# Attention backward for one query row: dq by 512-column matmuls in four column groups, with a diagonal pick

## The chip, the cores and the metric

One Trainium2 chip, one core of it, one launch. The metric is device time in microseconds (us). The kernel before takes 645.75 us, the median of three timed runs (645.3 to 645.95). Durations of single instructions come from one more execution that the hardware profiler recorded.

## The reference, cut to what matters

For each of 32 heads there is one query row q (128 numbers), 8192 rows of K and of V (128 numbers each, bfloat16), and one gradient row g. The kernel returns the output and the three gradients:

```
p  = softmax(K q * d^-0.5)          # 8192 numbers
o  = V^T p                          # 128 numbers
ds = p * (V g - g.o) * d^-0.5       # 8192 numbers
dq = K^T ds                         # 128 numbers  <- the change is here
dk = ds (x) q ,  dv = p (x) g       # 8192 x 128 each, written out
```

K and V are read once (134 MB in all) and dk and dv are written once (134 MB). There is little arithmetic for each byte.

## The kernel before, in words

The 8192 rows of a head lie on 128 partitions with 64 slots of 128 numbers each (`NT` = 64), so K of a head is one tile of 128 x 8192 bfloat16, 2 MB. One DMA loads it (line 74), one loads V (L78), and one each stores dk and dv (L225, cut in two for the first and last head). All of these are issued by SyncE (SP), in order, on one queue. K has three buffers, V two, the tiles G_dk and G_dv two each; so a load or a store that needs a buffer waits on SP for the last reader of that buffer, and everything behind it on SP waits too.

The order of the instructions on each engine is the order of the program (a manual schedule). Iteration h of the loop at L260 works on the scores of head h and ends head h-1. On TensorE (PE) it goes: L230 spreads the rows q and g over the partitions; L157 multiplies K, transposed by VectorE (DVE, L146), with q (64 weight loads of 128 columns and 64 matmuls); then come 32 matmuls of dq of head h-1 (L205, from `dq_of`, L245); L173 (`s_swap`) moves the scores into their order with four fp32 matmuls, each into its own 32 partitions; then the other 32 matmuls of dq; L288 transposes the maxima; L188 transposes V in four batches of eight; L300 sums the softmax; L205 (second use) multiplies V with p; L200 multiplies the transposed V with g; L320 computes g.o.

dq of a head is thus 64 pairs: a slot of K (128 x 128) is loaded as weights, and one column of ds streams past it, all 64 summed in column 128 of the PSUM tile `dp`. ScalarE (ACT) copies that column to `dq_all` (L249). ACT also computes the exponential (L299), copies p four times over (L309), and copies the transposed V out of PSUM (L179).

DVE transposes K (L146, four of 1.2 us), computes ds (L239, L241), masks the scores (L163), and builds dk and dv (L215, four pieces of 1.2 us each). `ds` and `p` are kept four times over (R = 4 copies side by side), since L215 reads them so; the tile `ds_rep` is 128 x 64 x 4. The pieces of dv of head h (first in L324) need p, which needs the sum from L300; ds of head h (L241, in the next iteration) needs L200 and L320.

Which instruction frees which buffer: the second half of dq (L278) is the last reader of K of head h-1, and load_k (L281) stands behind it; the transposes, the products with p and L200 free V, and load_v (L327) stands behind them. The PSUM tile `dp` has two buffers (`psD`, L57).

Of the kernel before, what the change touches and what calls it, by code (L numbers as in the profile page):

```python
# [9 lines left out]
ALU = mybir.AluOpType  # L10
AX = mybir.AxisListType
BF16 = mybir.dt.bfloat16
F32 = mybir.dt.float32
PSUM = bass.MemoryType.PSUM

CH = 16
R = 4
K_BUFS = 3
V_BUFS = 2
QD = 32  # L20
# [3 lines left out]
def kernel(  # L24
# [11 lines left out]
    nc = tc.nc  # L36
    P = 128
    _, H, S, D = k.shape
    assert D == P and S % (P * CH) == 0 and H <= P
    NT = S // P  # L40
    NCH = NT // CH
    NQ = P // QD
# [5 lines left out]
    consts = ctx.enter_context(tc.tile_pool(name="consts", bufs=1))  # L48
# [5 lines left out]
    small = ctx.enter_context(tc.tile_pool(name="small", bufs=2))  # L54
    psT = ctx.enter_context(tc.tile_pool(name="psT", bufs=2, space=PSUM))
    psS = ctx.enter_context(tc.tile_pool(name="psS", bufs=1, space=PSUM))
    psD = ctx.enter_context(tc.tile_pool(name="psD", bufs=2, space=PSUM))  # L57
    psM = ctx.enter_context(tc.tile_pool(name="psM", bufs=1, space=PSUM))

    Kt, Vt, XK, XV, st = {}, {}, {}, {}, {}  # L60

    def rows_of(x, h, c, parts):
        L = NT // parts
        return x[0, h].rearrange("(p n) d -> p n d", p=P)[:, c * L:(c + 1) * L, :]

    def slots(X, c, parts):
        L = NT // parts
        return X[:, c * L:(c + 1) * L, :]

    def load_k(h):  # L70
        Kt[h] = kpool.tile([P, NT, D], BF16, tag="K", name="Kt")
        parts = NCH if h == 0 else 1
        for c in range(parts):
            nc.sync.dma_start(slots(Kt[h], c, parts), rows_of(k, h, c, parts))
# [38 lines left out]
    nc.vector.reduce_sum(lane[:], ident[:].rearrange("p (a i) -> p i a", a=NQ), axis=AX.X)  # L113
    ident_f = consts.tile([P, P], F32)
    nc.vector.tensor_copy(ident_f[:], ident[:])
    for c in range(2 * NB):
        nc.vector.tensor_tensor(
            q_blk[:, :, c, :], tp[:, c, 0:H].unsqueeze(2).to_broadcast([P, H, NQ]),
            in_quad[:].unsqueeze(1).to_broadcast([P, H, NQ]), op=ALU.mult)
# [19 lines left out]
    dq_all = consts.tile([P, H], F32)  # L139

    def k_blocks(h, u):


        if u == 0:
            XK[h] = ktpool.tile([P, CH, NB, NCH, QD], F32, tag="XK", name="XK_sb")
        nc.vector.transpose(XK[h][:, :, :, u, :],  # L146
                            slots(Kt[h], u, NCH).rearrange("p g d -> p (g d)").bitcast(F32).rearrange(
                                "p (g w j) -> p g w j", g=CH, w=NB))

    def k_scores(h):  # L150
        x = st[h]
        out = x["s"][:, 0:NT].rearrange("p (a g) -> p g a", a=NQ)
        cols = XK.pop(h).rearrange("p g w u i -> p (g w u i)").bitcast(BF16).rearrange(
            "p (g w ui e) -> p g w e ui", g=CH, w=NB, e=2)
        for g in range(CH):
            for c in range(2 * NB):
                nc.tensor.matmul(out[:, g, :], lhsT=cols[:, g, c // 2, c % 2], rhs=q_blk[:, h, c, :],  # L157
                                 start=(c == 0), stop=(c == 2 * NB - 1), skip_group_check=True)
# [44 lines left out]
    def contract(Xt, rep, out_col, first=0, last=NT):  # L203
        for n in range(first, last):
            nc.tensor.matmul(out_col, lhsT=Xt[:, n, :], rhs=rep[:, n, 0:1],  # L205
                             start=(n == 0), stop=(n == NT - 1), skip_group_check=True)

    def outer(h, which, r):
        x = st[h]
        if r == 0:  # L210
            x[which] = gpool.tile([P, NT, D], BF16, tag=which, name="G_" + which)
        G, dst = x[which], out_2 if which == "dk" else out_3
        rep, row = x["ds"] if which == "dk" else x["p"], x["qd"][:, 0 if which == "dk" else 1, :]
        Q = NT // 4
        nc.vector.tensor_tensor(  # L215
            slots(G, r, 4).rearrange("p n (a b) -> p n a b", b=R),
            slots(rep, r, 4).unsqueeze(2).to_broadcast([P, Q, D // R, R]),
            row.rearrange("p (a b) -> p a b", b=R).unsqueeze(1).to_broadcast([P, Q, D // R, R]),
            op=ALU.mult)
        parts = 1  # L220
        if h == 0 or h == H - 1:
            parts = 2
        if r % (4 // parts) == 4 // parts - 1:
            c = r // (4 // parts)
            nc.sync.dma_start(rows_of(dst, h, c, parts), slots(G, c, parts))  # L225

    def rows_bc(h):
        x = st[h]
        x["s"] = psS.tile([P, 512], F32, tag="s", name="s_ps")
        nc.tensor.matmul(x["s"][:, 256:512], lhsT=ident[0:H, h:h + 1].to_broadcast([H, P]),  # L230
                         rhs=rows[:].rearrange("h a d -> h (a d)"), start=True, stop=True,
                         skip_group_check=True)
        x["qd"] = small.tile([P, 2, D], BF16, tag="qd", name="qd")
        nc.scalar.copy(x["qd"][:].rearrange("p a d -> p (a d)"), x["s"][:, 256:512])  # L234
# [8 lines left out]
            in1=x["p_s"][:].unsqueeze(2).to_broadcast([P, NT, R]), op0=ALU.subtract, op1=ALU.mult)  # L243

    def dq_of(h, half):  # L245
        out = st[h]["dp"][:, 128:129]
        contract(Kt[h], st[h]["ds"], out, half * NT // 2, (half + 1) * NT // 2)
        if half == 1:
            nc.scalar.copy(dq_all[:, h:h + 1], out)  # L249

    def result(src, dst):
        half = small.tile([P, H], BF16, tag="half", name="half")
# [7 lines left out]
    for h in range(H + 1):  # L260
        p_ = h - 1
        if h < H:
            x = st[h] = {}
            rows_bc(h)
            for u in range(NCH):
                k_blocks(h, u)
            k_scores(h)
        if h == 0:
            do_columns()
        if h > 0:  # L270
            ds_of(p_)
            outer(p_, "dk", 0)
            dq_of(p_, 0)
        if h < H:
            s_mask(h)
            s_swap(h)
        if h > 0:
            dq_of(p_, 1)  # L278
            outer(p_, "dk", 1)
        if 0 < h and h + 2 < H:  # L280
            load_k(h + 2)  # L281
        if h < H:
            mx = small.tile([P, 1], F32, tag="mx")
            nc.vector.reduce_max(mx[:], x["sn"], axis=AX.X)
            top = small.tile([P, 1], F32, tag="top")
            nc.vector.tensor_scalar_mul(top[:], mx[:], scale)
            x["m"] = psM.tile([P, 512], F32, tag="m", name="m_ps")
            nc.tensor.transpose(x["m"][:, 128:256], top[:].to_broadcast([P, P]), ident_f[:])  # L288
        if h > 0:
            outer(p_, "dk", 2)  # L290
        if h == 0:
            load_k(2)
        if h < H:
            nbias = small.tile([P, 1], F32, tag="nbias")
            nc.vector.tensor_reduce(nbias[:], x["m"][:, 128:256], axis=AX.X, op=ALU.max, negate=True)  # L295
            v_transposes(h, 0, copy=False)
            e = small.tile([P, NT], F32, tag="e")
            rs = small.tile([P, 1], F32, tag="rs")
            nc.scalar.activation(e[:], x["sn"], ACT.Exp, bias=nbias[:], scale=scale, accum_out=rs[:])  # L299
            nc.tensor.matmul(x["m"][:, 0:1], lhsT=ones_f[:], rhs=rs[:], start=True, stop=True,  # L300
                             skip_group_check=True)
        if h > 0:
            outer(p_, "dk", 3)
        if h == H:
            break
        rinv = small.tile([P, 1], F32, tag="rinv")
        nc.vector.reciprocal(rinv[:], x["m"][:, 0:1])  # L307
        x["p"] = small.tile([P, NT, R], BF16, tag="prep", name="p_rep")
        nc.scalar.activation(x["p"][:], e[:].unsqueeze(2).to_broadcast([P, NT, R]), ACT.Copy, scale=rinv[:])  # L309
        x["p_s"] = small.tile([P, NT], F32, tag="p_s", name="p_s")  # L310
        nc.vector.tensor_scalar(x["p_s"][:], e[:], rinv[:], scale, op0=ALU.mult, op1=ALU.mult)
        v_copy(h, 0)
        v_transposes(h, 1)
        v_transposes(h, 2)
        contract(Vt[h], x["p"], x["m"][:, 2:3])
        nc.scalar.copy(o_all[:, h:h + 1], x["m"][:, 2:3])
        v_scores(h, 0)
        v_scores(h, 1)
        v_transposes(h, 3)
        nc.tensor.matmul(x["m"][:, 1:2], lhsT=do_f[:, h:h + 1].to_broadcast([P, P]), rhs=o_all[:, h:h + 1],  # L320
                         start=True, stop=True, skip_group_check=True)
        v_scores(h, 2)
        v_scores(h, 3)
        outer(h, "dv", 0)  # L324
        outer(h, "dv", 1)
        outer(h, "dv", 2)
        if 0 < h and h + 2 < H:  # L327
            load_v(h + 2)
        outer(h, "dv", 3)
        if h == 0:  # L330
            load_v(2)
        if h == H - 1:
            result(o_all, out_0)
# [33 lines left out]
```

## Time and profile before

| what | value |
|---|---|
| three timed runs | 645.3, 645.75, 645.95 us |
| span of the profiled execution (first to last instruction) | 644.6 us |
| what lies around the span, against the median | about 1.15 us |
| busy: PE, PE weight load, DVE, ACT | 482.0, 443.9, 505.9, 180.7 us |
| TensorE clock granted, mean | 0.601 of full |
| bytes moved by DMA | 269.80 MB, mean 419 GB/s |
| dq: matmuls (L205 on `dp`) | 2048, 64.0 us busy |
| dq: weight loads (L205 on `Kt`) | 2048, 59.5 us busy |
| dq: copies (L249) | 32, 159 ns each |

The page does not give a time of the profiled execution beyond its span; the difference to the timed runs is taken as constant here. Busy times of PE are unions of overlapping instructions, so 2048 matmuls of 165 ns make 64 us and not 338. "Idle before" in a row is time in which the engine stood still just before such an instruction, and what ended it. "Landing" of a DMA is when its last byte is reported.

### The profile page before, as it was taken

How to read it: one execution, taken by the hardware profiler on the slowest of the kernel's cores; microseconds unless marked ns; L12 is line 12 of the kernel's file. 1: busy time of each engine (PE TensorE's matmuls, PEld its weight loads, DVE VectorE, ACT ScalarE, POOL GpSimd, SP SyncE). 2: the span in 40 equal slices, each digit the busy share in tenths (PEclk: the TensorE clock that was granted, in tenths of full speed). 3: DMA queues.
4: the chain of work that ended last, by engine and by line, in shares of the span. 5: the costliest groups of instructions: out<-in, count | busy, mean ns of one | idle time of the engine just before them, and what ended most of it. 6: DMA issues, size and time to landing. Idle time of an engine off the chain costs nothing.

```text
span 644.6 us, 20935 instructions
## 1 busy us (share of the span) xinstructions
PE 482.0 (75%) x9673; PEld 443.9 (69%) x9673; DVE 505.9 (78%) x653; ACT 180.7 (28%) x332; POOL 0.7 (0%) x6
## 2 busy tenths in 40 slices
PE   3998898886777877768776787677876777877780
PEld 2887788785676766768666687567776676866670
DVE  5999899767977679867788777787767986778761
ACT  2333333322233231333222332123322233231230
POOL 0000000000000000000000000000000000000000
PEclk9666666665566655666556665566665566655665
DMA  8999999999999999999999999999999999999985
GB/s 350 404 428 429 424 427 424 428 429 421 418 429 428 428 425 430 430 426 431 425 428 428 430 426 428 428 428 427 427 429 431 424 432 424 430 426 429 427 362 244
DMA packets 19718, 269.80 MB, mean 419 GB/s; under 512 B 2352, under 2 KB 2352, under 8 KB 2864
## 3 DMA queue, kind: packets, MB, share of 16 engines
q1 hardware_dynamic: 19584, 268.47, 98.2%
q8 instruction: 75, 1.23, 0.7%
q14 instruction: 11, 0.09, 0.0%
q10 hardware_dynamic: 48, 0.01, 0.0%
HBM read 134.23 MB, written 134.23 MB: 416 GB/s over the span
## 4 chain that ended last, share of the span: by engine, by line
DMA 62%; PE 24%; DVE 9%; ACT 1%; issue 1%; SPq 0%; DVEq 0%; ACTq 0%
DMA Vt<-in_v_dram 61%; PE T_ps L188 15%; DVE XK_sb L146 4%; DVE G_dv L215 4%; PE m_ps L205 3%; PE dp_ps L200 2%; PE s_ps L157 2%; PE dp_ps L205 1%; DVE G_dk L215 1%; DMA Kt<-in_k_dram 1%; PE m_ps L300 1%; ACT p_rep L309 0%; PE s_ps L173 0%; ACT XT_sb L179 0%; PE m_ps L288 0%
## 5 line engine op out<-in xcount | busy, mean ns | idle before, releaser
L188 PE MATMUL T_ps<-ident_f,Vt 128*128 128x128 f32 x1024 | 217.0, 383 | 27.3 <-DMA Vt<-in_v_dram 24.7
L188 PEld LDWEIGHTS T_ps<-ident_f,Vt 128*128 128x128 f32 x1024 | 182.2, 206 | 45.2 <-PE m_ps L288 21.7
L215 DVE TENSOR_TENSOR G_dv<-p_rep,qd 128x2048 bf16<-128x2048 bf16 x128 | 148.2, 1220 | 60.9 <-DMA out_dram<-G_dv 52.8
L215 DVE TENSOR_TENSOR G_dk<-ds_rep,qd 128x2048 bf16<-128x2048 bf16 x128 | 155.6, 1218 | 4.6 <-DMA out_dram<-G_dk 3.6
L146 DVE STREAM_TRANSPOSE XK_sb<-Kt 128x1024 f32<-128x1024 f32 x128 | 148.3, 1214 | 5.8 <-DMA Kt<-in_k_dram 3.2
L179 ACT COPY XT_sb<-T_ps 128x1024 f32<-128x1024 f32 x128 | 128.7, 1008 | 83.9 <-PE T_ps L188 77.2
L157 PE MATMUL s_ps<-q_blk,XK_sb 128*128 128x4 bf16 x2048 | 59.8, 168 | 94.6 <-DVE pdt L239 87.6
L157 PEld LDWEIGHTS <-XK_sb 128*128 128x128 bf16 x2048 | 57.1, 104 | 103.9 <-DVE pdt L239 96.6
L200 PE MATMUL dp_ps<-do_blk,XT_sb 128*128 128x2 bf16 x2048 | 67.0, 164 | 18.0 <-ACT XT_sb L179 17.6
L200 PEld LDWEIGHTS <-XT_sb 128*128 128x128 bf16 x2048 | 65.5, 103 | 20.7 <-ACT XT_sb L179 20.2
L205 PE MATMUL dp_ps<-ds_rep,Kt 128*128 128x1 bf16 x2048 | 64.0, 165 | 0.4 <-DVE ds_rep L241 0.4
L205 PEld LDWEIGHTS <-Kt 128*128 128x128 bf16 x2048 | 59.5, 104 | 5.7 <-issue 5.6
L249 ACT COPY dq_all<-dp_ps 128x1 f32<-128x1 f32 x32 | 5.1, 159 | 205.2 <-PE dp_ps L205 182.8
L205 PEld LDWEIGHTS <-Vt 128*128 128x128 bf16 x2048 | 57.0, 96 | 0.7
L205 PE MATMUL m_ps<-p_rep,Vt 128*128 128x1 bf16 x2048 | 56.5, 163 | 0.0
L309 ACT ACTIVATE p_rep<-e,rinv 128x256 bf16<-128x256 f32 x32 | 16.3, 508 | 64.6 <-DVE rinv L307 64.6
L307 DVE RECIPROCAL rinv<-m_ps 128x1 f32<-128x1 f32 x32 | 5.4, 168 | 35.2 <-PE m_ps L300 35.1
L234 ACT CAST qd<-s_ps 128x256 bf16<-128x256 f32 x32 | 11.9, 372 | 32.5 <-PE s_ps L230 32.5
L299 ACT ACTIVATE e<-s_ps,nbias 128x64 f32<-128x64 f32 x32 | 10.1, 314 | 32.5 <-DVE nbias L295 32.5
L241 DVE SCALAR_TENSOR_TENSOR ds_rep<-dp_ps,pdt,p_s 128x256 bf16<-128x256 f32 x32 | 15.5, 484 | 4.6 <-PE dp_ps L200 1.3
L163 DVE TENSOR_TENSOR sm<-s_ps,in_quad 128x256 f32<-128x256 f32 x32 | 13.6, 425 | 6.0 <-PE s_ps L157 2.0
L300 PEld LDWEIGHTS m_ps<-rs,ones_f 128*128 128x128 f32 x64 | 17.6, 334 | 0.0
(44 smaller groups left out, 153.1 us busy)
## 6 DMA issues: line engine op xcount, KB each, us to landing
Vt<-in_v_dram SPq DMA_DIRECT2D x32, 2048.0 KB, 30.1
Kt<-in_k_dram SPq DMA_DIRECT2D x31, 2048.0 KB, 30.3
out_dram<-G_dv SPq DMA_DIRECT2D x30, 2048.0 KB, 34.5
out_dram<-G_dk SPq DMA_DIRECT2D x30, 2048.0 KB, 33.7
out_dram<-G_dv SPq DMA_DIRECT2D x4, 1024.0 KB, 14.4
out_dram<-G_dk SPq DMA_DIRECT2D x4, 1024.0 KB, 13.2
Kt<-in_k_dram SPq DMA_DIRECT2D x4, 512.0 KB, 5.1
out_dram<-fin_sb SPq DMA_DIRECT2D x2, 8.0 KB, 12.8
```

The costliest lines, as they stand in the source:

```text
L146: nc.vector.transpose(XK[h][:, :, :, u, :], slots(Kt[h], u, NCH).rearrange("p g d -> p (g d)").bitcast(F32).rearrange("p (g w j) -> p g w ...
L157: nc.tensor.matmul(out[:, g, :], lhsT=cols[:, g, c // 2, c % 2], rhs=q_blk[:, h, c, :], start=(c == 0), stop=(c == 2 * NB - 1), skip_group ...
L163: nc.vector.tensor_tensor(x["sm"][:], x["s"][:, 0:NT].rearrange("p (a g) -> p a g", a=NQ).unsqueeze(2) .to_broadcast([P, NQ, NCH, CH]), in ...
L179: nc.scalar.copy(X[:], st[h].pop("T")[:])
L188: nc.tensor.transpose(T_ps[:, i, :], words[:, m * P:(m + 1) * P], ident_f[:])
L200: nc.tensor.matmul(st[h]["dp"][:, n:n + 2], lhsT=X[:, i, e2, :], rhs=do_blk[:, h, e2, :], start=(e2 == 0), stop=(e2 == 1), skip_group_chec ...
L205: nc.tensor.matmul(out_col, lhsT=Xt[:, n, :], rhs=rep[:, n, 0:1], start=(n == 0), stop=(n == NT - 1), skip_group_check=True)
L215: nc.vector.tensor_tensor(slots(G, r, 4).rearrange("p n (a b) -> p n a b", b=R), slots(rep, r, 4).unsqueeze(2).to_broadcast([P, Q, D // R, ...
L234: nc.scalar.copy(x["qd"][:].rearrange("p a d -> p (a d)"), x["s"][:, 256:512])
L241: nc.vector.scalar_tensor_tensor(out=x["ds"][:], in0=x["dp"][:, 0:NT].unsqueeze(2).to_broadcast([P, NT, R]), scalar=pdt[:], in1=x["p_s"][: ...
L300: nc.tensor.matmul(x["m"][:, 0:1], lhsT=ones_f[:], rhs=rs[:], start=True, stop=True, skip_group_check=True)
L309: nc.scalar.activation(x["p"][:], e[:].unsqueeze(2).to_broadcast([P, NT, R]), ACT.Copy, scale=rinv[:])
```

## The change

dq of a head no longer loads K as weights. The weights are now eight neighbouring slots of ds with their four copies each (128 x 32), and four slots of K (128 x 512) stream past them. The product has 32 rows: row 4k + r, columns 128 j to 128 j + 127 hold ds of slot k times K of slot j. Only k = j is wanted. There are 16 such matmuls to a head. Matmul g writes the 32 partitions of column group g mod 4, so neighbours use different column groups of the array, and each group sums four of them in a new PSUM tile of one bank (`psW`). In group 3 the wanted slots are k = 4 to 7, since the eight slots of ds start four earlier there, to stay inside the tile.

ACT copies the 128 x 512 fp32 sums to SBUF (`wide_out`), and four fp32 matmuls (`blocks`), each with a 128 x 128 block as weights and one column of a constant mask `diag` as the moving operand, pick the diagonal blocks and add the four groups, in the same column 128 of `dp` as before. `dq_of` keeps its two places in the loop, with eight wide matmuls each; the copy out stands at the end of the second; the four fp32 matmuls and the copy into `dq_all` stand later, after the third piece of dk (`dq_out`, ahead of the maxima's reduction at L295 and of the first transposes of V). `dp` has one PSUM buffer now instead of two. Two small DVE instructions build `diag` at the start.

```diff
-    psD = ctx.enter_context(tc.tile_pool(name="psD", bufs=2, space=PSUM))
+    wpool = ctx.enter_context(tc.tile_pool(name="wsb", bufs=2))
+    psD = ctx.enter_context(tc.tile_pool(name="psD", bufs=1, space=PSUM))
+    psW = ctx.enter_context(tc.tile_pool(name="psW", bufs=1, space=PSUM))
...
+    diag_low = consts.tile([P, R], F32)
+    nc.vector.reduce_sum(
+        diag_low[:], ident_f[:, 0:3 * QD].rearrange("p (a k r) -> p k r a", a=3, r=R)[:, 0:R, 0, :], axis=AX.X)
+    diag = consts.tile([P, R], F32)
+    nc.vector.tensor_tensor(
+        diag[:], diag_low[:], ident_f[:, 3 * QD + 4 * R:P].rearrange("p (k r) -> p k r", r=R)[:, :, 0], op=ALU.add)
...
+    def wide(h, which, first, last):
+        x = st[h]
+        Xt, rep = (Kt[h], x["ds"]) if which == "dq" else (Vt[h], x["p"])
+        if first == 0:
+            x["w"] = psW.tile([P, 512], F32, tag="w", name="w_ps")
+        for g in range(first, last):
+            a = g % NQ
+            n = 4 * g - (4 if a == NQ - 1 else 0)
+            nc.tensor.matmul(x["w"][a * QD:(a + 1) * QD, :], lhsT=rep[:, n:n + 2 * R, :].rearrange("p n r -> p (n r)"),
+                             rhs=Xt[:, 4 * g:4 * g + 4, :].rearrange("p n d -> p (n d)"),
+                             start=(g < NQ), stop=(g >= NT // 4 - NQ), skip_group_check=True)
+
+    def wide_out(h):
+        x = st[h]
+        x["wsb"] = wpool.tile([P, 4, D], F32, tag="wsb", name="w_sb")
+        nc.scalar.copy(x["wsb"][:].rearrange("p k d -> p (k d)"), x.pop("w")[:])
+
+    def blocks(h, out_col):
+        X = st[h].pop("wsb")
+        for k in range(R):
+            nc.tensor.matmul(out_col, lhsT=X[:, k, :], rhs=diag[:, k:k + 1],
+                             start=(k == 0), stop=(k == R - 1), skip_group_check=True)
...
     def dq_of(h, half):
+        wide(h, "dq", half * NT // 8, (half + 1) * NT // 8)
+        if half == 1:
+            wide_out(h)
+
+    def dq_out(h):
         out = st[h]["dp"][:, 128:129]
-        contract(Kt[h], st[h]["ds"], out, half * NT // 2, (half + 1) * NT // 2)
-        if half == 1:
-            nc.scalar.copy(dq_all[:, h:h + 1], out)
+        blocks(h, out)
+        nc.scalar.copy(dq_all[:, h:h + 1], out)
...
         if h > 0:
             outer(p_, "dk", 2)
+            dq_out(p_)
```

## The prediction

> **What bounds the kernel now.** I read the page's slices and queues, then the chain of waits in order of time, then one head as a timeline, then the records of DMA packets and landings.
>
> ```profile
> PE 482.0 (75%) x9673; PEld 443.9 (69%) x9673; DVE 505.9 (78%) x653; ACT 180.7 (28%) x332; POOL 0.7 (0%) x6
> DMA  8999999999999999999999999999999999999985
> q8 instruction: 75, 1.23, 0.7%
> ```
>
> No engine is over 78% busy, while the DMA row is full from the second slice to the last but two: the transfers bound the kernel, and an engine's time counts only where it makes them stop. The chain (start, duration, what) shows that engines once paced the heads:
>
> ```profile
> 33.47 4.63 DVE G_dv L215 x4
> ...
> 49.85 4.63 DVE G_dv L215 x4
> ...
> 542.86 30.88 DMA Vt<-in_v_dram
> ...
> 583.15 31.02 DMA Vt<-in_v_dram
> ```
>
> Early, dv of one head follows that of the last after 49.85 - 33.47 = **16.38 us**: that is what the engines need for a head. Late, two heads take 583.15 - 542.86 = 40.3 us, **20.1 us** each, and V takes 31 us from issue to landing: a deep queue. So the engines have over 3 us per head to spare.
>
> What does a head cost the queue? In the trace's landings, most 2 MB transfers land 4.86 us after the one before; four make 19.44 us. Some take longer, and they are not random. Numbering the 75 instruction packets of queue q8 (16,384 bytes each) from 0, the landing just after every eighth is late:
>
> ```
> packet   0: 17.72   next landing  20.25, 6.28 after the one before
> packet   8: 76.43                 81.88, 6.38
> packet  16: 135.50               141.66, 6.37
> packet  24: 205.46               211.53, 6.22
> packet  32: 273.65               276.20, 6.29
> packet  40: 335.94               340.89, 6.36
> packet  48: 405.44               410.39, 6.37
> packet  56: 473.12               475.24, 6.53
> packet  64: 541.40               544.58, 6.13
> packet  72: 607.35               609.45, 6.55
> ```
>
> Only three other full transfers are over 5.1 (5.95, 5.36, 5.16). My reading: the packets go round eight of the 16 DMA engines, each delays its engine, and a transfer has landed when the slowest has finished. The engine hit first in each round stays the latest, and its delay adds up: ten times 6.35 - 4.86, less what next landings give back, about **1.45 us** each. The end supports it (stretch, length, four engines' busy time, clock, DMA share, GB/s):
>
> ```profile
> 633.00:637.00 4.00, 0.00 (x0) 0.00 (x0) 0.00 (x0) 0.00 (x0) 0.00 (x0) 0.50 0.68 282
> 637.00:641.00 4.00, 0.00 (x0) 0.00 (x0) 0.00 (x0) 0.00 (x0) 0.00 (x0) 0.50 0.52 218
> ```
>
> With nothing left to issue, about half of the DMA engines still work: the others are done some ten us before. So the end is set by the bytes plus the instruction packets on the latest engine.
>
> **The change, part by part.** The stage in a head that only the engines paced:
>
> ```profile
> 78.91 0.99 PE L205 MATMUL dp_ps<-ds_rep,Kt 128*128 128x1 bf16 x32
> 79.83 0.44 PE L173 MATMUL s_ps<-sm,lane 128*32 128x64 f32 x8
> 80.20 1.01 PE L205 MATMUL dp_ps<-ds_rep,Kt 128*128 128x1 bf16 x32
> 81.25 0.16 ACT L249 COPY dq_all<-dp_ps 128x1 f32<-128x1 f32 x1 [4.60 <-PE dp_ps L205]
> 81.36 1.91 PE L188 MATMUL T_ps<-ident_f,Vt 128*128 128x128 f32 x8
> 83.07 0.42 PE L300 MATMUL m_ps<-rs,ones_f 128*128 128x1 f32 x2
> 83.53 0.17 DVE L307 RECIPROCAL rinv<-m_ps 128x1 f32<-128x1 f32 x1
> 84.34 4.63 DVE L215 TENSOR_TENSOR G_dv<-p_rep,qd 128x2048 bf16<-128x2048 bf16 x4 [0.27 <-ACT p_rep L309]
> ```
>
> - Removed: 64 pairs, 0.99 + 1.01 = **2.0 us** of PE per head.
> - Added, 16 wide matmuls. One of 256 columns (L230) takes 391 ns, one of 4 (L157) 168: 0.885 ns a column, so 0.62 us for 512, and a next one in the same group 512 x 0.885 = 0.45 later. Do four groups run together? L173 uses them: eight matmuls of 313 ns in 0.44. In the records four start within 20 ns, and the second four 105 ns after the first. Eight in a row would take 106 ns each (L188: 213 ns from one 128-column fp32 matmul to the next; half for 64), 0.85 + 0.2. So they do: a half is 0.62 + 0.45 = 1.07, both **2.1 us**. One after another it would be 16 x 0.45 = **7.2**. I take 2.1, by the row that uses the same groups.
> - Added, the ACT copy. 1 column takes 159 ns (L249), 1024 take 1008 (L179): 0.58 us for 512, about 0.66 with a signal before and after.
> - Added, four fp32 picks. L300 is the same form: from its first matmul (83.07) to the next batch's (83.36) 0.29 us. Four make 1.15, the first load 0.2: **1.35 us**. By bounds from bf16 pairs (27 ns) and whole L300 groups (0.42), 0.1 to 1.7.
> - Moved: PE waits in order for that copy, and behind it are V's transposes, L300, and through them p and dv. L188 starts 0.14 + 0.66 + 1.35, less the 0.1 that it now waits, or **2.0 us** later. `dq_all`'s copy now holds up the exponential, but that ends before L300 comes up. K's release (line 281 behind the second half) moves 0.1 us. One buffer of `dp` costs nothing: its reader L249 ends before L188, L200 comes over 4 us later.
>
> Sum for a head that the engines pace: 16.4 + 2.0 = **18.4 us**; the queue needs 19.44 and the late landings. So the queue stays full and hides it all; early heads only fill it more slowly. If this cover goes (a head over about 19.8 us), each us costs 31. The last head starts its transposes about 2 us later at most, but the last store, issued at 630.40, lands at 643.38, 13 us behind its issue, and dq's last DMA, issued about 2 us later than 630.82, still waits behind it. DVE's two constants (under 0.7 us, by the 349 ns of L113) and 32 more ACT instructions are beside the initial loads and in ACT's 72% idle time.
>
> **What is left is the instruction packets.** A head has 604 PE instructions (19,346 / 32, weight loads counted). The change takes 128 and adds 32 for the wide ones and 4 x 4 for the picks (L300 shows 2 + 2 for one): 80 fewer, 2560 in all. One packet serves 256 (16,384 bytes; 1.23 MB / 19,346 = 64 bytes each), so exactly ten fall away: 65 instead of 75. The latest engine gets numbers 0, 8, ..., 64: nine, not ten. Packet k came when PE had started 256k + 190 to 256k + 442 instructions, so number 64 is asked for at 16,574 or later of some 16,800: it comes, around 620 us, with stores still to go. Gain: one delay, **1.45 us**. Last landing 643.54 - 1.45 = 642.1, span 643.15; with 1.15 around it as before, **644.3 us**.
>
> The Trainium skill ("Runtime: NRT & Kernel Launch", Instruction fetch mechanics) says that instructions are fetched in blocks of 16 KiB, which the 75 rows agree with, and that crossing a block is mostly hidden. By that rule my gain is nil: the second rival. The ten late landings speak against it.
>
> **Rivals.**
> 1. *Groups one after another* (slower). Weight loads of a group wait for the matmul in flight. With 7.2 us in place of 2.1, a head takes 18.4 + 5.1 = 23.5, 3.7 over the queue's 19.8; 31 heads: **760 us**. With pairs only (eight steps of 0.45, and 0.17) 20.1, so 31 x 0.3: about **655**. It decides from 19.8 us. For it: no row has 512 columns in a group. Against it: L173. The Trainium skill ("TensorE: Matmul & The Clock Gate", Part 3, What overlaps and what doesn't) says that weight loads overlap running matmuls only when their row groups differ; all four groups here use the same rows. By that rule this rival would hold; L173's second four loads start 28 ns after the first matmuls, so the trace does not agree.
> 2. *Nothing moves.* The late landings only accompany the packets (something else that returns every 66 us): **645.75**. Against it: each eighth fits, though 66 us is constant too.
> 3. *Two delays fall away.* If packet 64 is not asked for: 645.75 - 2.9 = **642.85**. Only some 230 instructions decide.
> 4. *The picks or the copy cost far more* than rows say: same point as 1, at 1.4 us more; counted with it.
>
> **How the numbers follow.** Forecast (engines hidden, one delay fewer) 74%, rival 2 10%, rival 3 6%, rivals 1 and 4 together 10%. A measurement here can tell 0.2%, or 1.3 us, from no change; 1.45 is just beyond, and runs scatter by 0.65 us, so of the 74 I give 52 to faster and 22 to no change. Faster 52 + 6 = 58%, same 22 + 10 = 32%, slower 10%. The range holds the forecast and rivals 2 and 3 with scatter, 642.6 to 646.2, and leaves out the slower tenth.
>
> **What would show it.** Right: 65 packets in q8; late landings after every eighth, about every 76 us (66 x 604 / 524); DMA full; wide matmuls starting in fours, 0.45 us apart; L188 waiting 2 us longer. Wrong: starts 0.4 us apart one by one, DMA slices under 9, or late landings still 66 us apart, which would make rival 2 true.

## The result and the profile after

The changed kernel takes **648.94 us** (median of four runs, 648.72 to 649.15) beside 645.85 for the kernel before in the same comparison: ratio 1.0047, 95% interval 1.0034 to 1.0061. It is 3.1 us slower; 1.45 us faster was forecast.

The page of the changed kernel, the rows that answer to those of before:

```profile
PE 537.8 (83%) x8393; PEld 456.8 (71%) x8393; DVE 506.1 (78%) x655; ACT 196.1 (30%) x364; POOL 0.7 (0%) x6
DMA  8999999999999999999999999999999999999984
q8 instruction: 65, 1.06, 0.6%
```

The DMA row is as full as before, and ten instruction packets are gone, as forecast. From the timeline of one early head (start, duration, engine, line, operation, tiles, count):

```profile
83.52 1.04 PE L226 MATMUL w_ps<-Kt,ds_rep 128*32 128x512 bf16 x8
...
84.56 1.07 PE L226 MATMUL w_ps<-Kt,ds_rep 128*32 128x512 bf16 x8
...
85.68 0.58 ACT L233 COPY w_sb<-w_ps 128x512 f32<-128x512 f32 x1 [4.58 <-PE w_ps L226]
...
86.32 1.86 PE L239 MATMUL dp_ps<-diag,w_sb 128*128 128x1 f32 x8 [0.21 <-ACT w_sb L233]
...
88.05 1.95 PE L197 MATMUL T_ps<-ident_f,Vt 128*128 128x128 f32 x8
```

Eight wide matmuls take 1.04 to 1.07 us: the four groups do run together. The picks take 1.86 us, half a microsecond more than forecast, and V's transposes wait for them. The chain of waits, in its early part:

```profile
35.38 4.63 DVE G_dv L249 x4
53.94 4.63 DVE G_dv L249 x4
```

dv of one head follows that of the last after 18.56 us (16.38 before, 18.4 forecast). So the engines behave as forecast, and the queue stays full. The surprise is at the end. Stretches of the tail of the kernel before, and then of the changed one (stretch, length, five engines, clock, DMA share, GB/s):

```profile
641.00:643.00 2.00, 0.00 (x0) 0.00 (x0) 0.00 (x0) 0.00 (x0) 0.00 (x0) 0.50 0.15 62
643.00:645.00 2.00, 0.00 (x0) 0.00 (x0) 0.00 (x0) 0.00 (x0) 0.00 (x0) 0.50 0.00 0
```

```profile
641.00:643.00 2.00, 0.00 (x0) 0.00 (x0) 0.00 (x0) 0.00 (x0) 0.00 (x0) 0.50 0.08 33
643.00:645.00 2.00, 0.00 (x0) 0.00 (x0) 0.00 (x0) 0.00 (x0) 0.00 (x0) 0.50 0.07 29
```

One of 16 engines is a share of 0.0625. In the kernel before two engines finish at about 643, and a third at 641.97; in the changed one a **single DMA engine** works on for two microseconds more. The trace gives no engine's number with a packet; an engine is followed here as a chain of packets, each of which starts where the one before ended. The ends of the chains say the same: 643.07, 642.92, 641.97 and then 640.9 before; 645.27, 641.92 and 639.95 after. In the kernel before, the chain that ends at 643.07 contains the packet behind instruction packet 72 (607.35 us), and the one at 642.92 shows the clusters of slow packets that are described next. So the engines that carry instruction packets did come earlier, by 1.15 us (643.07 to 641.92). A ninth engine, which the prediction did not see, came 2.2 us later than the old end.

What delays it? Of the packets of 16,384 bytes, 97% take 611 to 621 ns. On this engine some take 625 to 770, in clusters. Here are two heads of the changed kernel, PE's rows from the timeline:

```profile
167.20 1.75 PE L214 MATMUL m_ps<-p_rep,Vt 128*128 128x1 bf16 x64
168.82 0.94 PE L209 MATMUL dp_ps<-do_blk,XT_sb 128*128 128x2 bf16 x32
```

```profile
342.05 1.75 PE L214 MATMUL m_ps<-p_rep,Vt 128*128 128x1 bf16 x64
343.67 0.98 PE L209 MATMUL dp_ps<-do_blk,XT_sb 128*128 128x2 bf16 x32
```

The work is the same. Beside the first, three packets come 150, 155 and 141 ns late; beside the second none does. The first pair of rows lies between the landings at 166.01 (K) and 171.46 (dk), so this engine carries the dk store; the second lies between 341.17 (dv) and 346.05 (K), so it carries the load of K. In the second head the late packets begin when the next store does (37, 80 and 61 ns from 346.19 on). This gave the theory that the later experiments test: **the engine loses some 5 ns for each matmul that starts while it carries a store, and next to nothing while it carries a load.** Each matmul brings a weight load of its own, and no run separates the two.

### The profile page after: what moved, and what is told of

Its sections match the earlier page's. It is cut to its first block, busy times and chain, and to the rows that moved or that the text cites. A ratio compares the mean times of both kernels' runs of the same rounds, so it can differ in the third digit from the quotient of the medians.

```text
span 646.9 us, 18408 instructions
## 1 busy us (share of the span) xinstructions
PE 537.8 (83%) x8393; PEld 456.8 (71%) x8393; DVE 506.1 (78%) x655; ACT 196.1 (30%) x364; POOL 0.7 (0%) x6
## 4 chain that ended last, share of the span: by engine, by line
DMA 49%; DVE 24%; PE 22%; ACT 2%; issue 1%; SPq 0%; ACTq 0%; DVEq 0%
DMA Kt<-in_k_dram 49%; DVE XK_sb L155 15%; DVE G_dv L249 8%; PE s_ps L166 6%; PE w_ps L226 6%; PE T_ps L197 4%; PE dp_ps L239 3%; ACT w_sb L233 1%; ACT p_rep L348 1%; PE s_ps L182 1%; PE m_ps L339 0%; DVE rinv L346 0%; PE m_ps L214 0%; PE dp_ps L209 0%; SPq L76 0%
## 5 line engine op out<-in xcount | busy, mean ns | idle before, releaser
L197 PEld LDWEIGHTS T_ps<-ident_f,Vt 128*128 128x128 f32 x1024 | 187.5, 212 | 11.9 <-ACT XT_sb L188 11.8
L249 DVE TENSOR_TENSOR G_dv<-p_rep,qd 128x2048 bf16<-128x2048 bf16 x128 | 148.2, 1220 | 30.9 <-DMA out_dram<-G_dv 27.8
L188 ACT COPY XT_sb<-T_ps 128x1024 f32<-128x1024 f32 x128 | 128.5, 1008 | 84.0 <-PE T_ps L197 80.0
L233 ACT COPY w_sb<-w_ps 128x512 f32<-128x512 f32 x32 | 18.7, 585 | 170.5 <-PE w_ps L226 170.5
L239 PEld LDWEIGHTS dp_ps<-diag,w_sb 128*128 128x128 f32 x256 | 57.0, 327 | 17.2 <-ACT w_sb L233 17.2
L226 PE MATMUL w_ps<-Kt,ds_rep 128*32 128x512 bf16 x512 | 67.3, 628 | 0.4 <-DVE ds_rep L275 0.4
L239 PE MATMUL dp_ps<-diag,w_sb 128*128 128x1 f32 x256 | 59.7, 355 | 7.2 <-ACT w_sb L233 7.1
L326 PEld LDWEIGHTS m_ps<-ident_f,top 128*128 128x128 f32 x32 | 5.8, 182 | 29.1 <-DVE top L324 29.1
L182 PEld LDWEIGHTS s_ps<-sm,lane 128*32 128x32 f32 x256 | 10.4, 151 | 17.6 <-DVE sm L172 16.7
```

The source lines that it names most:

```text
L182: nc.tensor.matmul(x["s"][a * QD:(a + 1) * QD, 128:128 + NT], lhsT=lane[:], rhs=x["sm"][:, a].rearrange("p u g -> p (u g)"), start=True, s ...
L188: nc.scalar.copy(X[:], st[h].pop("T")[:])
L197: nc.tensor.transpose(T_ps[:, i, :], words[:, m * P:(m + 1) * P], ident_f[:])
L226: nc.tensor.matmul(x["w"][a * QD:(a + 1) * QD, :], lhsT=rep[:, n:n + 2 * R, :].rearrange("p n r -> p (n r)"), rhs=Xt[:, 4 * g:4 * g + 4, : ...
L233: nc.scalar.copy(x["wsb"][:].rearrange("p k d -> p (k d)"), x.pop("w")[:])
L239: nc.tensor.matmul(out_col, lhsT=X[:, k, :], rhs=diag[:, k:k + 1], start=(k == 0), stop=(k == R - 1), skip_group_check=True)
```

## The experiments

The first four were made before that theory stood; "path" means that a head takes longer because PE waits.

**late_picks**: the picks and dq's copy moved to where PE is idle, behind the scores of V of the next head.

```diff
             outer(p_, "dk", 2)
-            dq_out(p_)
+            if h == H: dq_out(p_, st[p_]["dp"][:, 128:129])
...
         v_scores(h, 3)
+        if h > 0: dq_out(p_, x["m"][:, 3:4])
```

> The changed kernel, with its four fp32 picks and the copy into dq_all moved behind the last product with g (L200's place in the iteration), where PE waits for K's transpose anyway; they write a free column of the tile of the sums. The trace of the changed kernel shows 65 instruction packets, as predicted, but its landings lose 0.45 us per head evenly instead of 1.45 at every eighth packet: a ninth DMA engine, which loses 0.15 to 0.25 us around the DMA issues, has become the latest. Theory 1 (path): that engine is later because the picks delay PE by 2 us per head and with it the issues; without the delay the time comes back to 644.4 to 645.8. Theory 2 (streaming): the wide matmuls themselves, or ACT's copy, slow the transfers; then the place of the picks does not matter and it stays at 648.5 to 649.2.

646.88 us (before: 646.09), ratio 1.0011, 1.0003 to 1.002. That is between the two theories: some 2.1 to 2.3 of the 3.1 us come back. Its latest engine ends at 642.97, the next at 640.82: the packet engines are 2 us ahead of the end, and still the ninth decides.

**before_delay**: the kernel before with four constant fp32 matmuls (result not used) where the picks stand.

```diff
             outer(p_, "dk", 2)
+            if h < H:
+                for _ in range(4):
+                    nc.tensor.matmul(x["m"][:, 4:5], lhsT=ident_f[:], rhs=ident_f[:, 0:1], start=True, stop=True, ...)
```

> The kernel before, with four fp32 matmuls of one column at the place where the change has its picks, from constants, with no copy to wait for; they compute nothing that is used. They delay V's transposes and all behind them on PE by about 1.8 us per head, as in the changed kernel (period of the early heads 18.1 us instead of 16.4), and bring two packets (77). Theory 1 (path): 648 to 649. Theory 2 (streaming): 645.6 to 646.

647.95 us, ratio 1.0028, 1.0017 to 1.0039: 1.9 us for the delay alone, with no wide matmul. The ninth engine ends at 644.16, the next at 641.86. So "hidden" was wrong by about 2 us, although the queue never ran dry.

**before_pad80**: the kernel before with 80 idle bf16 pairs a head (result not used), where PE stands still.

```diff
         v_scores(h, 3)
+        for _ in range(80):
+            nc.tensor.matmul(x["m"][:, 4:5], lhsT=ident[:], rhs=ident[:, 0:1], start=True, stop=True, ...)
```

> The kernel before, with 80 more bf16 pairs of one column in each head, behind the last product with g, where PE is idle (2.1 us; 3 us are idle in the phase that the transfers pace). They compute nothing that is used. 160 more PE instructions per head make 5120, or 20 more instruction packets, 95 in all: twelve on the first of the eight engines instead of ten. If a packet costs its engine 1.45 us and that engine is the latest, 2.9 us more: 648.7. If packets cost nothing: 645.8.

660.05 us, ratio 1.0214, 1.02 to 1.0228: 14 us, not three. 95 packets came, as the count asks, but they are not the price: one engine ends at 656.96, the other fifteen by 648.77. Early heads do grow, to 18.0 to 18.6 us; in before_delay, where they take 18.0 to 19.2, that cost 1.9 us. My packets (2.9 us) and a longer path together leave 9 of the 14 us unexplained.

**after_stores_act**: the changed kernel with all stores of dk and dv issued by ACT.

```diff
-            nc.sync.dma_start(rows_of(dst, h, c, parts), slots(G, c, parts))
+            nc.scalar.dma_start(rows_of(dst, h, c, parts), slots(G, c, parts))
```

> The changed kernel with the stores of dk and dv issued by ACT instead of SyncE, at the same places of the program; the loads stay on SyncE. If the ninth engine's loss belongs to the queue that issues, it is now shared between two queues, and the eight engines with the packets are the latest again: 644 to 645.5, with late landings at every eighth packet. If the loss belongs to the transfers as such, 648.9.

653.61 us, ratio 1.0108, 1.0094 to 1.0121: worse than either expectation. Its tail:

```profile
645.00:647.00 2.00, 0.00 (x0) 0.00 (x0) 0.00 (x0) 0.00 (x0) 0.00 (x0) 0.50 0.24 90
647.00:649.00 2.00, 0.00 (x0) 0.00 (x0) 0.00 (x0) 0.00 (x0) 0.00 (x0) 0.50 0.07 29
649.00:651.00 2.00, 0.00 (x0) 0.00 (x0) 0.00 (x0) 0.00 (x0) 0.00 (x0) 0.50 0.06 25
```

Fifteen engines end within 0.15 us of each other (645.43 to 645.58), and one works on alone until 651.11. So a second queue did not share out the lag; it grew from 3.4 us in the changed kernel (645.27 beside 641.92) to 5.5. The other engines end later too. The pieces of dv and dk wait longer for the stores of two heads earlier (DVE's waits: who, for whom, total us, times, longest):

```profile
DVE G_dv L249 <- DMA out_dram<-G_dv: 38.6, 20, 2.0
DVE G_dk L249 <- DMA out_dram<-G_dk: 9.0, 21, 1.1
```

In the changed kernel it is 27.8 for dv, and dk's pieces have 1.1 us of idle time in all. What part of the loss these waits make was not tried. The run is useful for another reason: with the stores in a queue of their own, the slow packets (624 to 800 ns, from 40 to 600 us) can be sorted. Beyond 611 ns they sum to 16.5 us among the stores and 4.4 among the loads.

**before_dv_first**: two issues exchanged, nothing added.

```diff
-        if 0 < h and h + 2 < H:
-            load_v(h + 2)
         outer(h, "dv", 3)
-        if h == 0:
-            load_v(2)
+        if h + 2 < H:
+            load_v(h + 2)
```

> The kernel before with one exchange in SP's queue: the dv store of a head is issued ahead of the load of V instead of behind it; no instruction is added. Theory A (from the slow packets of the six traces so far): one of the sixteen DMA engines loses about 5 ns for every matmul that TensorE starts while that engine carries a store, and next to nothing while it carries a load. In the kernel before the stores lie in the first 5 us and in the third 5 us after a landing of V, with 51 matmuls a head; after the exchange they would lie from 5 to 15 us, with 147. 96 more at 5 ns are 0.48 us a head, over 22 to 28 heads 10.6 to 13.4 us: 656.5 to 659.5 us beside about 646. Theory B (the engine loses time around the issues of DMAs, or for every instruction wherever it falls): the issues and instructions are the same, only 0.4 us later: 645.8 to 646.8.

**670.51 us** (before: 645.96), ratio 1.038, 1.0365 to 1.0394. The theory gave the direction and half the size: the order also moved PE against the transfers, so that the scores of K (64 matmuls) fell into a store as well. Its own tail:

```profile
661.00:663.00 2.00, 0.00 (x0) 0.00 (x0) 0.00 (x0) 0.00 (x0) 0.00 (x0) 0.50 0.06 25
663.00:665.00 2.00, 0.00 (x0) 0.00 (x0) 0.00 (x0) 0.00 (x0) 0.00 (x0) 0.50 0.07 29
```

A share of 0.06 is one engine, for 5 us. It ends at 665.58, the others by 660.48. They too end 17 us or more later than in the kernel before: from 400 to 600 us all engines together move 409 to 410 GB/s here, against 428 there. That fits engines that must wait for the latest one, since a transfer has landed only when its slowest engine has finished.

**pad40_store** and **pad40_load**: 40 idle pairs a head (result not used) at two places, first beside the dk store, then beside the load of V.

```diff
         v_scores(h, 3)
+        for _ in range(40):
+            nc.tensor.matmul(x["m"][:, 4:5], lhsT=ident[:], rhs=ident[:, 0:1], start=True, stop=True, ...)
```

```diff
             outer(p_, "dk", 0)
+            for _ in range(40):
+                nc.tensor.matmul(st[p_]["dp"][:, 132:133], lhsT=ident[:], rhs=ident[:, 0:1], start=True, stop=True, ...)
             dq_of(p_, 0)
```

> The kernel before with 40 idle bf16 pairs (28 ns each, their result is not used) a head behind the last scores of V, where TensorE stands still 2.4 us and the DMA engines carry the dk store. Theory A: 40 pairs at 4.3 ns (the slope of the 80 pairs) are 0.17 us a head, over 32 heads 5.5 us: 651 to 653 us. A price only through instruction packets (5 more, 10 in all on eight engines): 647.5 to 648.5.

> The same 40 idle pairs ahead of the first half of dq, where the DMA engines carry the load of V once the queue is deep; here they also make TensorE's path up to 1.1 us longer a head. Theory A: the pairs themselves cost almost nothing, some ten others are pushed into the next store (0.05 us a head, 1.2 us) and the longer path costs about 1 us in the first 200 us: 647 to 648.8 us, 3 to 5 us under the other place. Theory B (each instruction costs wherever it falls): as much as the other place or more, 651 to 654.

650.92 us (ratio 1.0077, 1.0064 to 1.009) and 649.85 (1.0061, 1.0048 to 1.0073). The first is at the lower edge of what the theory gave; the second is a microsecond over, and the two lie 1.1 us apart where 3 to 5 were expected. In the times alone this is a miss. The landings tell more: V's landing near 197 us comes 2.6 us later than in the kernel before with the pairs beside the load, and 1.6 with the pairs beside the store; the last landing of all comes 3.4 and 4.6 later. So once the queue is deep the place beside the store costs 2.2 us more, 0.1 us a head, and the early part, where the place beside the load costs a microsecond more, hides half of it.

**after_no_picks**: the changed kernel without copy, picks and dq (dq is left out).

> The changed kernel without the copy of the wide result, the four picks and the copy of dq (dq is left out of the output): the 64 pairs are gone and the path is not longer. The prediction's own step (fewer instruction packets move the end): 644.6 on a chip where the kernel before takes 646.1. Theory A: the packets of eight engines fall off as there, but the ninth engine is as late as before, since the removed pairs lay beside loads: 645.5 to 646.7.

645.37 us, ratio 0.999, 0.9981 to 0.9999. Without the picks there are 63 packets, twelve fewer than before. These and no longer path are worth 0.6 us, where the prediction's step gave at least 1.45: the ninth engine ends at 642.47, the next at 640.85. The 1.4 us between this run and late_picks (by the ratios) were not taken apart.

**before_scores_early** and **late_scores_early**: the kernel before, and the one with late picks, each with 16 score pairs moved out of the dk store, ahead of the transposes.

```diff
         v_scores(h, 1)
+        v_scores(h, 2)
         v_transposes(h, 3)
...
-        v_scores(h, 2)
         v_scores(h, 3)
```

> The kernel before with the third sixteen score pairs of V ahead of the last eight transposes instead of behind them; nothing is added. Theory A: these 16 pairs move from the dk store into the load of K in front of it; half of the eight transposes moves the other way; 12 matmuls a head at 5 ns are 0.06 us, 1.3 to 1.9 us on the ninth engine by the end. The engines that carry instruction packets ended as late as it in the kernel before (643.07 us in its trace), so little of it shows: 645.4 to 646.1 us beside 646.0. If the ninth engine does not set the end, no change: 646.0.

> The same move in the changed kernel with late picks (646.9 us). Its packet engines ended at 640.8 us and the ninth alone at 642.96. Theory A: the ninth comes 1.3 to 1.9 us earlier and what the fewer packets bring shows at last: 645.0 to 645.7 us, under the kernel before. If moving 16 pairs by 1 us does nothing: 646.9.

645.80 us (before: 645.84; ratio 1.0, 0.9991 to 1.0009) and **645.65** (0.9994, 0.9985 to 1.0004). In the kernel before nothing shows; that fits packet engines that end with the ninth, but without the theory no change was expected either, so this run decides nothing. In the other, at 1.0011 without this move, it gives about 1.1 us. This is the best form of the change that I found, and it cannot be told from the kernel before.

**late_first_heads** and **late_other_heads**: late picks only in the first 12 heads, or only in the others (the diff, against late_picks, is the first; the other has h > 12 in both lines).

```diff
-            if h == H: dq_out(p_, st[p_]["dp"][:, 128:129])
+            if h == H or not (h <= 12): dq_out(p_, st[p_]["dp"][:, 128:129])
...
-        if h > 0: dq_out(p_, x["m"][:, 3:4])
+        if h > 0 and h <= 12: dq_out(p_, x["m"][:, 3:4])
```

> The changed kernel with the picks and the dq copy moved behind the scores of V in the first 12 heads alone (to about 250 us), at the changed kernel's place in the others. Theory A: the longer path costs time only while the queue of transfers is still filling (the landings of the two kernels drift apart by 1.9 us up to 217 us and not after), so nearly all of what the late picks gave comes back here: 646.7 to 647.3 us, beside 646.9 with all of them late and 648.9 with none. If a longer path costs the same in every head, 12 of 32 heads give 0.8 us back: 648.1.

> The reverse: late picks from the 13th head on, the changed kernel's place in the first 12. Theory A: 648.5 to 649.1 us, as the changed kernel. If a longer path costs the same in every head, 20 of 32 give 1.3 us back: 647.6.

647.07 us (ratio 1.0015, 1.0006 to 1.0025) and 648.78 (1.0039, 1.0026 to 1.0051). The longer path costs in the first 12 heads, and in the others half a microsecond at most, which the intervals do not tell from nothing. Landings of V in the changed kernel, and how much earlier the same landing is in two others:

```
changed kernel   us from issue   late_picks   late_first_heads
     115.8           18.4          -0.6           -0.3
     155.2           20.8          -0.3           -0.0
     196.8           25.3          -1.6           -1.2
     236.8           28.2          -1.9           -1.4
     316.3           29.6          -1.9           -1.5
     515.8           30.2          -2.2           -1.4
```

The gap opens between 155 and 237 us, while the time from issue to landing in the changed kernel grows from 21 to 28 us, and then hardly moves.

**pad80_small** and **pool_memsets** ask what the engine loses time to: the 80 pairs with weights of 32 x 32 (result not used), and 5000 memsets of one column on GpSimd that nothing waits for.

```diff
+            nc.tensor.matmul(x["m"][0:32, 4:5], lhsT=ident[0:32, 0:32], rhs=ident[0:32, 0:1], start=True, stop=True, ...)
...
+    idle = consts.tile([P, 1], F32)
+    for _ in range(5000):
+        nc.gpsimd.memset(idle[:], 0.0)
```

> The kernel before with 80 idle pairs a head at the place of the 80 larger ones, with weights of 32 x 32 in place of 128 x 128 (their result is not used). If the engine that carries stores loses time for each instruction that TensorE starts, whatever it reads: as with the larger ones, 658 to 661 us. If it loses it to what TensorE reads from SBUF (a quarter of the rows and columns): 647 to 652.

> The kernel before with 5000 memsets of one column (about 100 ns each) on GpSimd from the start, which nothing waits for; they take about 500 us. If an instruction of any engine costs the storing engine 5 ns: half of them fall beside stores, 2500 times 5 ns, 12.5 us: about 658 us, seen in the trace as store packets of 625 to 800 ns. If only TensorE's instructions do: 646 us, or as much more as the packets of GpSimd's own instructions (5000 times 64 bytes, 320 KB) delay the latest engine, seen in the trace as whole packets and not as slow ones.

662.06 us (ratio 1.0248, 1.0227 to 1.0268; before: 645.63): small weights cost as much as large ones, so it is not the weights that TensorE reads. The second kernel's 784.71 us are no answer, because the memsets come 156 ns apart and outlast all else (its page: line, engine, operation, tile, count, busy, mean ns, idle before):

```profile
L93 POOL MEMSET idle<- 128x1 f32 x5000 | 492.1, 98 | 288.8
```

Its transfers answer: the ninth engine ends at 648.65 us beside 643.07, and a store of it is 275 ns late with 25 matmuls and some 32 memsets in it. By the table below 25 matmuls make about 170; the rest is 3.3 ns for each memset. It does not come from instruction packets, of which queue q14 has 50 here and 11 before: stores with one of them and stores without are late alike (medians 279 and 265 ns). So GpSimd's instructions cost it as well, by this one run.

All of it in one table: how late a transfer of the latest engine lands (beyond the 4.863 us of eight plain packets and a signal), and how many matmuls start in it, means over the stretch given:

```
kernel, us                store: matmuls, ns late   load: matmuls, ns late
late_picks, 140-600              29   187                 103   39
changed, 240-600                 31   201                 100   37
pad40_load, 200-600              32   189                 139   36
pad40_store, 200-600             46   258                 125   22
changed, 140-230                 64   349                  74   86
before_pad80, 100-600            81   437                 114   31
before_dv_first, 100-600        125   611                  26   39
```

Stores follow a line: 611 - 187 over 125 - 29 is 4.4 ns a matmul. Single stores of one run follow it too: in pad80_small those with 20 to 23 matmuls are 80 to 170 ns late, those with 115 to 120 are 550 to 660. Loads follow none: 139 matmuls cost no more than 26, and the one high value (86) comes from one load of nine, 0.6 us late, behind an instruction packet at 160.31 us.

## Why the prediction was wrong, point by point

- *The transfers bound the kernel.* Right, in every run with one queue but pool_memsets, which its memsets end.
- *An instruction packet delays its engine by about 1.45 us, and eight engines take them in turn.* Right: the packet engines of the changed kernel ended 1.15 us earlier. But a sign that was named for it did not come: with packets as far apart as forecast (every eighth after 69 to 80 us), the landing behind packet 8 was late (6.27), and those behind the seven others took 4.9 to 5.5. Another engine was already the slowest.
- *"So the end is set by the bytes plus the instruction packets on the latest engine."* **This step failed.** A ninth engine loses time on each store (0.20 to 0.35 us in the changed kernel) to the matmuls that start beside it. In the kernel before it kept pace with the packet engines, which is why the late landings fitted so well; with fewer packets on the others it alone set the end. Of the 1.45 us, after_no_picks shows 0.6.
- *"So the queue stays full and hides it all; early heads only fill it more slowly."* **This failed too**, by 1.9 to 2.3 us. The queue stayed full, but how fast it fills decides where PE's dense matmuls lie beside the transfers. A head of 16.4 us slides quickly against the 19.9 of the queue, one of 18.56 slowly, and it stays longer where its matmuls meet stores: in the changed kernel 64 matmuls per store from 140 to 230 us, and 31 later. Nine stores 138 ns later (349 less the 211 of late_picks in the same stretch) make 1.2 us, and nine loads 59 later (86 less 27) 0.5; together they are the gap in the landings. The part of the loads is the one behind an instruction packet and not a matter of matmuls. late_first_heads and late_other_heads show it from the other side.
- *Wide matmuls 2.1 us, copy 0.58.* Right: 1.04 + 1.07, and 0.585. The Trainium skill ("TensorE: Matmul & The Clock Gate", Part 3, What overlaps and what doesn't) says that weight loads overlap matmuls in flight only when row groups differ; here all use the same rows, the second four loads start while the first four matmuls run, and eight of 628 ns take 1.04 us, so the trace does not agree.
- *Picks 1.35 us.* Mis-sized: 1.86. The four matmuls run as eight passes, each with a weight load, that start 213 ns apart, the step that the prediction itself read for L188; the 0.29 us for a pair of passes came from a pair alone. It made a head 18.56 and not 18.4 us.
- *What lies around the span, 1.15 us.* It is 1.7 to 2.0 in all later runs (before: spans of 643.5 to 645.0); the profiled execution of before was one of the longer ones.
- *Rival 2, nothing moves.* Its time of 645.75 was nearer than the forecast, for another reason: the packets do delay their engines, but another engine was as late, and the longer path made it later. The Trainium skill ("Runtime: NRT & Kernel Launch", Instruction fetch mechanics) calls the crossing of a 16 KiB block mostly hidden; the 1.15 us by which those engines came earlier speak against it, and so does after_no_picks, though only by 0.6 us of the 1.45 that I took.

**What stays open.** Why that engine? The Trainium skill ("NOTIFIC — the notification-queue block", section 12.3, The AWS profiler on NQ 0) says that the profiler has start and end of the instructions of all five engines recorded, into a ring in HBM. Such writes would fit the pattern: instructions of TensorE and of GpSimd alike, with small weights or large, and only beside stores, which also write to memory. Every execution here, the timed ones too, has a recorded span, so no run shows whether the loss would be there without recording, and the cause is argued, not shown.

## What to carry to other kernels

Where the DMA row is full, ask which of the 16 engines ends last and what else it does: a DMA share of 0.06 to 0.07 in the tail is one engine, and a gain on the others is worth nothing. "Hidden behind the transfers" has to be read as well as a question of timing: a step that stops nothing can still slide the engines against the transfers, and while the queue was filling that cost 2 us here. The order of two issues in one queue can be worth more than the computation that is being tuned: 24.5 us against 3.

## What the hardware showed beyond that

- One DMA engine lost 4.4 ns on its stores for each matmul (with its weight load), and in one run 3.3 for each GpSimd memset, started in that time; loads lost next to nothing (36 ns with 139 matmuls).
- Exchanging the dv store and the load of V in SP's queue, mostly 0.43 us apart in the kernel before, cost 3.8%.
- Issuing stores from a second queue brought 15 engines within 0.15 us of each other and left the sixteenth 5.5 us behind; it took longer than the changed kernel: 1.0108 of the kernel before against 1.0047.
- 32-row weights made 80 idle pairs no cheaper: 662.06 us against 660.05 in another comparison.
